# A linear-attention and GLU block: attention pinned in one order, k and v in thirds, single PSUM banks, and a logarithm for the root

## The chip, the cores and the metric

The kernel runs on one core of one Trainium2 chip. The metric is device time in microseconds (us) of one execution.

## The reference

Sequence 2048, model width 576, 32 heads of 18, GLU width 4608, all in fp32:

```python
xn = layernorm(x)                                  # 2048 x 576
q, k, v = split(xn @ wqkv)                         # 32 heads of 18 each
phi = lambda t: jnp.where(t > 0, t + 1, jnp.exp(t)) + 1e-6
pq, pk = phi(q), phi(k)
kv = einsum("bhsd,bhse->bhde", pk, v)              # per head 18 x 18
z = einsum("bhsd->bhd", pk)
o = (pq @ kv) / (pq . z + 1e-6)
s = merge_heads(o) @ wo
glu = (gelu(x1 @ w_gate) * (x1 @ w_up)) @ w_down   # x1 = xn
out = x + s * silu(glu)
```

## The kernel before

**Tiles and words.** The 2048 tokens are 4 blocks of 512 (TBN), each of 4 tiles of 128 (so tiles 0 to 15; `2 * TT` is 8). The width 576 is cut in two halves of 288, a half in two chunks of 128 rows and a rest of 32. Every operand of a big product is held as two words: the high word is a copy rounded to fp32r by ScalarE (Copy), the low word is what is left, subtracted by VectorE or GpSimd. A product of one half then takes the seven matmuls of PASSES (high x high, high x low and low x high of both chunks, and one for the rests).

**Attention, first part.** `moments` (L141) makes mean and 1/sqrt(variance) of one to four tiles: statistics on VectorE, a Sqrt on ScalarE (L153), a reciprocal and one Newton step on VectorE. `center` normalizes a tile in place, `turn` (L169) transposes it on TensorE, six 128x128 pieces into a pair of PSUM banks (xt), `place` (L178) writes the words (xo) and keeps an fp32 copy (xf). k and v of a tile (`k_mm`, `v_mm`, through `mm_x` L315) are 28 matmuls of 288 columns each into a pair of banks (pk, pv). `k_post` forms phi(k): VectorE's minimum, ScalarE's Exp, VectorE's maximum, GpSimd's sum. `v_post` copies v, head group by head group with a column of ones, into va, partly on VectorE and partly on ScalarE, and then runs `kv_mm` (L306) of the tile before, which adds va^T pk of five head groups to the banks kv_a and kv_b. This part, tiles 0 to 7, is written out by hand from L984 on; `fixed[0]` is true, so every engine keeps the order of the program.

**Attention, second part.** From `fixed[0] = False` on, ScalarE, VectorE and TensorE instructions are ordered by the framework's scheduler, not by the program; GpSimd's `pool` and the `dma` calls stay pinned. Here the kernel makes the differences T1 to T4 of the halves of x (for the Winograd products of the GLU), stores their words in DRAM (`keep`), makes q of blocks 0 and 1 (`q_store`, five groups a block, 14 matmuls of 512 columns each at L374, phi, to DRAM), normalizes blocks 2 and 3 (`norm`), makes k and v of tiles 8 to 15, and q of blocks 2 and 3 (`q_hold`, kept on chip). `kv_done` and `kv_wo` fold the output weights wo into kv (kvh, kvl, kv4). `make_sel` writes a selection matrix; `den` (L553) makes the denominators of a block and their reciprocals, `scale` spreads them over the heads with a matmul (b, L565), multiplies q by them (ph, L567) and makes the words pq. `s_mm` (L588) is 28 matmuls of 288 a tile; s goes to DRAM.

**GLU.** `fixed[0]` is true again. 36 matrices (18 gate, 18 up, in turn) each make seven products into eight banks: al, be, ga and de for two blocks at a time (`matrix`, L669 is the matmul of `product`); the words of the next matrix (wa, wb) are cut behind them in the `todo` lists. Then `down_all` makes the down projection in 126 groups of 24 matmuls (bd, L874) from words of h (s, by `prep_s`) and of the down weights (t), with seven Winograd steps into eight banks, and `close` applies silu, multiplies by s, adds x and stores.

**PSUM.** A pool of `n1` single banks and `n2` pairs is opened for each stage: `banks(0, 3)` at first, (2, 2) from the differences on, (4, 2) for the q of block 3 and s, and (8, 0) for the GLU; two more banks hold kv_a and kv_b until (4, 2) is opened.

The helpers `act` (L97), `vec` (L100), `mm` (L103) and `pool` (L106) record most operations, so these four lines stand for many places and the operand names tell them apart.

Of the kernel before, what the change touches and what calls it, by code (L numbers as in the profile page):

```python
# [36 lines left out]
LN_EPS = 1e-5  # L37
EPS = 1e-6
# [12 lines left out]
def block_kernel(ctx, tc, x, xe, wq_d, wkv_d, wo, wgu_d, wd_d, out):  # L51
# [53 lines left out]
    def pool(op, *args):  # L105
        tc.keep_in_program_order(getattr(nc.gpsimd, op)(*args))  # L106
# [4 lines left out]
    def split(hi, lo, src):  # L111
        nc.scalar.activation(hi, src, AF.Copy)
        nc.vector.tensor_sub(lo, src, hi.bitcast(F32))
# [26 lines left out]

    def moments(tb, t0=0, t1=TT):  # L141
        n = t1 - t0
        bn = sb.tile([P, TT, 12], F32, tag="bn", bufs=2, name=f"bn_{tb}_{t0}")
        st = sb.tile([P, 6, TT], F32, tag="st", bufs=4, name=f"st_{tb}_{t0}")
        mv = sb.tile([P, 2 * TT, 2], F32, tag="mv", bufs=4, name=f"mv_{tb}_{t0}")
        for t in range(t0, t1):
            xs = xstat[tb, t // 2 * 2][:, t % 2]
            for j in range(2):
                vec("bn_stats", out=bn[:, t - t0, 6 * j : 6 * j + 6], in_=xs[:, j, 0:HALF])
            vec("bn_aggr", out=mv[:, t - t0, :], in_=bn[:, t - t0, :])  # L150
        sd, v, r, c = (st[:, i, 0:n] for i in range(4))
        var = mv[:, 0:n, 1]
        act(sd, var, AF.Sqrt, bias=eps_t)  # L153
        vec("tensor_scalar", v, var, LN_EPS, None, op0=ALU.add)
        vec("reciprocal", r, sd)
        vec("tensor_mul", c, r, r)
        vec("tensor_mul", c, c, v)
        vec("tensor_scalar", c, c, -0.5, 1.5, op0=ALU.mult, op1=ALU.add)
        vec("tensor_mul", c, c, r)
        for t in range(t0, t1):  # L160
            mom[tb * TT + t] = mv[:, t - t0, 0:1], c[:, t - t0 : t - t0 + 1]

    def center(n):

        xs = xstat[n // TT, n % TT // 2 * 2][:, n % 2]
        m, r = mom.pop(n)
        vec("tensor_scalar", xs, xs, m, r, op0=ALU.subtract, op1=ALU.mult)

    def turn(n):  # L169

        xs = xstat[n // TT, n % TT // 2 * 2][:, n % 2]
        xts[n] = pair(f"xt_{n}")
        for j in range(2):
            for k in range(3):
                c = slice(k * P, (k + 1) * P)
                pin(nc.tensor.transpose(xts[n][:, j, c], xs[:, j, c], ident))  # L176

    def place(n):  # L178

        tb, t = divmod(n, TT)  # L180
        s, b = divmod(tb, 2)
        c = slice(t * P, (t + 1) * P)
        for j, nm in enumerate(BS[b]):
            if t == 0:
                xo[s][nm] = big(2 * b + j, [P, 5, TBN], F32R, f"xo_{s}_{nm}")
            o = xo[s][nm]
            v = xts[n][:, j, 0 : 3 * P].rearrange("p (k t) -> p k t", k=3)
            act(o[:, 0:3, c], v, AF.Copy)
# [20 lines left out]
    def norm(tb):  # L209
        moments(tb)  # L210
        for n in range(tb * TT, tb * TT + TT):
            center(n)
            turn(n)
            place(n)

    def differences(s, eng):
        f = xf[s]
        eng.tensor_sub(f["B11"], f["B12"], f["B11"])
        f["T1"] = f["B11"]
        eng.tensor_sub(f["B12"], f["B22"], f["B12"])  # L220
# [13 lines left out]
    def build(s, nm, i):  # L234
        o = big(i, [P, 5, TBN], F32R, f"xo_{s}_{nm}")
# [5 lines left out]
    wsub = {}  # L241

    NC2 = (Q2, HALF, HALF)

    def w_tiles(mats, first, name):
        n, nc2 = 2 * len(mats), 2 * NC2[mats[0]]
        mains = [big(first + i, [P, 4, nc2], F32R, f"{name}_{i}") for i in range(n)]
        last = big(first + n, [P, n, nc2], F32R, f"{name}_l")
        for i, m in enumerate(mats):
            for j in range(2):  # L250
                wsub[m, j] = (mains[2 * i + j], last[:, 2 * i + j, :])

    def load_w(m, c, j):
        raw = slot([P, 3, HALF], F32, f"rw_{m}_{c}_{j}")
        nc.sync.dma_start(out=raw, in_=wkv_d[2 * m - 2 + c, j])
        return raw

    def load_w2(m, j, i):
        raw = big(i, [P, 2, 3, NC2[m]], F32, f"rw_{m}_{j}")
        src = wq_d[:, j] if m == 0 else wkv_d[2 * m - 2 : 2 * m, j]  # L260
        nc.sync.dma_start(out=raw, in_=src.rearrange("c p k f -> p c k f"))
        return raw[:, 0], raw[:, 1]

    def prep_hi(m, c, j):
        act(wsub[m, j][0][:, 0:3, c * NC2[m] : (c + 1) * NC2[m]], raws[m, c, j], AF.Copy)

    def prep_lo(m, c, j, on_pool):
        main, last = wsub[m, j]
        cs = slice(c * NC2[m], (c + 1) * NC2[m])
        r = slice(2 * KR, 3 * KR)  # L270
        raw = raws[m, c, j]
# [43 lines left out]
    def mm_x(o, m, tb, t, js=(0, 1)):  # L315
        s, b = divmod(tb, 2)
        for j in js:
            for i, (wi, xi, rows) in enumerate(PASSES):
                for c in range(2):
                    mm(  # L320
                        o[:, c, 0:HALF],
                        xo[s][BS[b][j]][0:rows, xi, t * P : (t + 1) * P],
                        w_part(m, j, wi, c * HALF, (c + 1) * HALF, rows),
# [650 lines left out]
    for t in (2, 3):  # L974
        load_stat(0, t)
# [206 lines left out]
```

## Time and profile before

| | |
|---|---|
| runs | 1549.44, 1551.21, 1551.27 us, median 1551.21 |
| the profiled execution | 1550.36 us; span of its instructions 1548.7 us |
| instructions | 22597 |
| mean granted TensorE clock | 0.993 of full speed |
| DMA | 257.36 MB in 112335 packets, mean 166 GB/s |

PE is TensorE's matmul, PEld its weight load, DVE VectorE, ACT ScalarE, POOL GpSimd, SP the engine that issues most DMAs. A row of groups has line, engine, operation, output <- inputs, shapes and count, then busy us and mean ns of one, then the idle time just before these instructions and what ended most of it. A row of waits has engine, what waited, what it waited for, then total us, count and the longest. A row of a timeline has start and length in us and a count. A window's row gives start:end, length, busy time (count) of each engine, the granted clock, the DMA engines' busy share and GB/s. In the order's rows a name ends in the number of its tile.

### The profile page before, as it was taken

To read this page: it belongs to the slowest core of one execution; us is meant where nothing else is said; L and a number is where in the kernel's file an instruction comes from. 1 tells how busy PE (TensorE), PEld (TensorE's weight loads), DVE (VectorE), ACT (ScalarE), POOL (GpSimd) and SP (SyncE) were. 2 spreads that over 40 slices of the span, in tenths; PEclk is the share of its full clock that TensorE was granted. 3 is DMA by queue.
4 is the path that set the end of the run, shared out by engine and by line. 5 is a ranking of instruction groups with operands and counts; after the bars stand their busy time and mean duration, and the time that the engine had idled before them with its cause. 6 is when DMAs were issued, how large, how long until landed. Compare 5 with 4: busy or idle time off the path is not lost.

```text
span 1548.7 us, 22597 instructions
## 1 busy us (share of the span) xinstructions
PE 1507.1 (97%) x8552; PEld 1343.1 (87%) x8552; DVE 1075.0 (69%) x1571; ACT 553.6 (36%) x945; POOL 563.8 (36%) x512
## 2 busy tenths in 40 slices
PE   4989999999999999999999999999999999999998
PEld 4988997888888888888888888888889999999998
DVE  6668336637777887877788787777784666555775
ACT  3435214333222222232232223232335545445443
POOL 4144423023456565444665554456440020000120
PEclk9999999999999999999999999999999999999999
DMA  4327000572344434333444343334569757787872
GB/s 153 135 89 263 4 6 2 184 269 111 133 158 167 167 131 162 120 129 128 165 166 165 133 154 114 133 135 167 197 224 323 248 168 253 246 266 242 285 251 105
DMA packets 112335, 257.36 MB, mean 166 GB/s; under 512 B 10130, under 2 KB 38546, under 8 KB 110178
## 3 DMA queue, kind: packets, MB, share of 16 engines
q1 hardware_dynamic: 110162, 243.07, 44.0%
q0 software_dynamic: 2064, 12.85, 2.3%
q8 instruction: 67, 1.10, 0.3%
q14 instruction: 42, 0.34, 0.1%
HBM read 157.93 MB, written 97.91 MB: 165 GB/s over the span
## 4 chain that ended last, share of the span: by engine, by line
PE 90%; DVE 6%; ACT 2%; DMA 1%; issue 1%; POOL 0%; SPq 0%; ACTq 0%; DVEq 0%; POOLq 0%
PE bd L874 25%; PE al L669 15%; PE de L669 15%; PE ga L669 15%; PE be L669 7%; PE s L588 4%; PE q L374 3%; PE pv L103 2%; PE pk L103 2%; PE kv_a L103 1%; DVE xo_B L100 1%; PE xt L176 1%; PE d L546 1%; DVE x L100 1%; DVE bn L100 1%
## 5 line engine op out<-in xcount | busy, mean ns | idle before, releaser
L874 PE MATMUL bd<-t,s 128*128 128x288 f32 x3024 | 401.4, 295 | 2.2 <-DVE u L100 2.2
L874 PEld LDWEIGHTS bd<-t,s 128*128 128x128 f32 x3024 | 400.9, 188 | 2.8 <-DVE u L100 2.7
L100 DVE TENSOR_TENSOR s<-sr,s 128x512 fp32r<-128x512 f32 x252 | 181.3, 759 | 119.5 <-ACT s L97 115.0
L97 ACT ACTIVATE s<-sr 128x512 fp32r<-128x512 f32 x252 | 149.2, 626 | 192.4 <-PE bd L874 125.4
L106 POOL TENSOR_TENSOR hs<-h,h 128x512 f32<-128x512 f32 x72 | 100.6, 1406 | 232.5 <-DVE h L100 229.6
L97 ACT ACTIVATE h<-h 128x512 f32<-128x512 f32 x108 | 67.0, 633 | 247.9 <-DVE h L100 132.5
L106 POOL TENSOR_TENSOR sx<-sx 128x288 f32<-128x288 f32 x24 | 27.9, 1182 | 318.6 <-DVE sx L100 317.5
L100 DVE TENSOR_TENSOR wa<-raw,wa 128x256 fp32r<-128x256 f32 x72 | 78.2, 1087 | 53.2 <-ACT wa L97 52.0
L106 POOL TENSOR_TENSOR sm<-raw 128x384 f32<-128x384 f32 x72 | 76.1, 1057 | 96.2 <-DMA raw<-in_wgu_dram 73.5
L100 DVE TENSOR_TENSOR h<-h,u 128x512 f32<-128x512 f32 x108 | 97.8, 905 | 3.7
L106 POOL TENSOR_TENSOR td<-td 128x288 f32<-128x288 f32 x72 | 72.4, 1005 | 55.4 <-DMA td<-in_wd_dram 51.1
L97 ACT ACTIVATE wa<-sm 128x1152 fp32r<-128x1152 f32 x36 | 41.8, 1161 | 139.2 <-PE de L669 139.2
L100 DVE TENSOR_TENSOR wa<-sm,wa 128x768 fp32r<-128x768 f32 x72 | 65.3, 907 | 35.7 <-ACT wa L97 34.9
L100 DVE TENSOR_TENSOR wb<-sm,wb 128x256 fp32r<-128x256 f32 x72 | 60.8, 844 | 20.5 <-ACT wb L97 20.0
L97 ACT ACTIVATE u<-al 128x512 f32<-128x512 f32 x72 | 40.9, 593 | 91.1 <-PE al L669 91.1
L100 DVE TENSOR_TENSOR wb<-raw,wb 128x256 fp32r<-128x256 f32 (+1 forms) x108 | 70.0, 648 | 1.7 <-ACT wb L97 0.2
L374 PE MATMUL q<-xo_B,wq 128*128 128x512 f32 x240 | 66.7, 404 | 1.6 <-ACT e_q L97 1.5
L100 DVE TENSOR_TENSOR u<-u,ga 128x512 f32<-128x512 f32 x72 | 49.3, 685 | 21.5 <-PE ga L669 20.4
L669 PE MATMUL al<-xo_B,wa 128*128 128x512 f32 x252 | 63.1, 390 | 0.8 <-ACT s L593 0.8
L669 PE MATMUL al<-xr_B,wa 128*128 128x512 f32 x252 | 63.0, 389 | 0.0
L669 PE MATMUL be<-xo_T,wa 128*128 128x512 f32 x252 | 63.0, 389 | 0.0
L669 PE MATMUL be<-xr_T,wa 128*128 128x512 f32 x252 | 63.0, 389 | 0.0
(176 smaller groups left out, 2973.0 us busy)
## 6 DMA issues: line engine op xcount, KB each, us to landing
sr<-hs SPq DMA_DIRECT2D x252, 256.0 KB
hs<-h SPq DMA_DIRECT2D x68, 512.0 KB
raw<-in_wgu_dram SPq DMA_DIRECT2D x36, 768.0 KB
hs<-hs SPq DMA_DIRECT2D x102, 256.0 KB
td<-in_wd_dram SPq DMA_DIRECT2D x18, 576.0 KB
td<-td SPq DMA_DIRECT2D x18, 576.0 KB
tr<-td SPq DMA_DIRECT2D x16, 576.0 KB
tr<-in_wd_dram SPq DMA_DIRECT2D x12, 576.0 KB
```

Of the source, the lines that this page charges most:

```text
L97: pin(nc.scalar.activation(*args, **kw))
L100: pin(getattr(nc.vector, op)(*args, **kw))
L103: pin(nc.tensor.matmul(*args, **kw))
L106: tc.keep_in_program_order(getattr(nc.gpsimd, op)(*args))
L176: pin(nc.tensor.transpose(xts[n][:, j, c], xs[:, j, c], ident))
L374: nc.tensor.matmul(pq, w_part(0, j, wi, gi * P, (gi + 1) * P, rows), xo[s][nm][0:rows, xi, :], start=(n == 0), stop=(n == 2 * len(PASSES) ...
L546: nc.tensor.matmul(pd[2 * H * i : 2 * H * (i + 1), 0:HB], at["zc"][:, gi, :], ph[tb][:, gi, i * HB : (i + 1) * HB], start=(gi == 0), stop= ...
L588: nc.tensor.matmul(pss[:, c, 0:HALF], pq[:, t * P : (t + 1) * P], kw[:, c * HALF : (c + 1) * HALF], start=(n == 0), stop=(n == len(steps) ...
L669: nc.tensor.matmul(o, w[0:rows, wi, :], xop[0:rows, xi, :], start=(start and n == 0), stop=(n == len(PASSES) - 1), skip_group_check=True,)
L874: nc.tensor.matmul(banks[j][:, 0:HALF], hw[n, s][:, a, t * P : (t + 1) * P], w[:, c, g % 4], start=(new and g == 0 and m == 0), stop=(g == ...
```

## The change

All of attention is written in one pinned order, and `fixed` is gone. In parts:

- **PSUM**: one pool for the whole kernel, six single banks (`bank`) and two more (`own_bank`), which hold the first transposes, then kv_a and kv_b, then al and two of the eight bd.
- **Root**: 1/sqrt(v) is exp(-0.5 ln v), then the same Newton step. `moments` is split in `spread` (statistics, Ln, Exp) and `scales` (the step). The table set that holds both functions is loaded by an instruction at the program's start.
- **Start**: 16 transposes of the identity stand ahead of everything on TensorE. Loads, words and products of tiles 0 and 1 are interleaved anew.
- **k and v** are made together in thirds of 384 columns, each third in one bank: `x_mm(t, c)` is 14 matmuls; the rest rows have a word of their own (KV_PASSES). The copies to va are all on ScalarE. `kv_tile` fixes the order within a tile: the next tile's transposes and words behind the first two thirds, `kv_mm` of the tile before behind the last third, normalizing of the tile after next at the end. `kv_mm(7)` stands behind the first q, `kv_mm(15)` behind the first q of block 2.
- **q of blocks 0 and 1**: behind each of the ten q's a list (`behind`) of what goes on: T4, the words of T1, T3, T2, and x of tiles 8 to 10. For block 3 the minimum in phi is made on ScalarE (Relu(-x), then Exp(-x)).
- **kv_wo** is run group by group between the q's of block 2; the moving of rows between its results has its own step.
- **s**: the words of q of the next block (`den`, `scale`, and now `halve`) are made between the tiles of s of the block before (`aside`); the odd blocks' words have buffers of their own (12 and 14). The words of block 3's and 1's T's and the sums and first words of the first gate matrix are also laid between tiles of s. T3 is read back behind the last s on GpSimd's queue, B21, B22 and T4 on SP's.
- **GLU**: the words wa and wb have exchanged buffers (15 and 14); the call `prep_s(3)`, in the last matrix, is moved from step 5 of the matrix to step 6. At the end `close_last` makes the sum and silu of a tile, and its product, addition and store stand behind the sum of the next; the last tile is done in two parts.
- **Host**: the weights of k and v are cut in three parts of 384 columns.

```diff
-        act(sd, var, AF.Sqrt, bias=eps_t)
...
-        vec("reciprocal", r, sd)
+        act(st[:, 0, 0:n], mv[:, 0:n, 1], AF.Ln, bias=eps_t)
+        act(st[:, 2, 0:n], st[:, 0, 0:n], AF.Exp, scale=-0.5)
...
+    def kv_tile(t, mid_=(), end=()):
+
+        ahead = t % (2 * TT) != 2 * TT - 1
+        x_mm(t, 0)
+        if ahead:
+            turn(t + 1)
+        k_post(t, 0)
+        x_mm(t, 1)
+        if ahead:
+            place(t + 1)
+            save(t + 1)
+        run(list(mid_))
+        k_post(t, 1)
+        v_post(t, 1)
+        x_mm(t, 2)
+        if t - 1 in vas:
+            kv_mm(t - 1)
+        run(list(end))
+        v_post(t, 2)
...
+    behind = {
+        0: [lambda: kv_mm(N0 - 1), lambda: difference(0, 3)],
+        1: [lambda: spread(N0, 2)],
+        2: [lambda: scales(N0), lambda: center(N0)],
+        3: [lambda: form("T1")],
+        4: [lambda: turn(N0), lambda: place(N0)],
+        5: [lambda: form("T3"), lambda: save(N0)],
+        6: [lambda: center(N0 + 1)],
+        7: [lambda: spread(N0 + 2, 2), lambda: scales(N0 + 2)],
+        8: [lambda: form("T2")],
+        9: [],
+    }
+    for i in range(2 * NHG):
+        q_store(*divmod(i, NHG))
+        run(behind[i])
...
+    aside = {
+        (2, 0): [lambda: den(3), lambda: build(1, "T1", X_SLOT["T1"])],
+        (2, 1): [lambda: scale(3, 0, 1), lambda: halve(3, 0, 1)],
+        (2, 2): [lambda: scale(3, 2, 3, 4), lambda: halve(3, 2, 3, 4)],
+        (2, 3): [lambda: build(1, "T3", X_SLOT["T3"]), lambda: load_mat(0), lambda: q_load(1, 8)],
+        (3, 0): [lambda: den(0), lambda: build(1, "T2", X_SLOT["T2"])],
...
+    for tb in (2, 3, 0, 1):
         for t in range(TT):
             s_mm(tb, t)
+            run(aside.get((tb, t), []))
...
-            todo[5] += [lambda: load_t(3), lambda: prep_s(3)]
+            todo[5].append(lambda: load_t(3))
+            todo[6].append(lambda: prep_s(3))
```

What TensorE gets first, before (xt are the transposes of a tile, pk the products of k, wkv the weights' words, xo_B x's words; the number behind tells the tile):

```order
L176 MATMUL xt_135<-ident,x_0_103 128x128 x6
L176 MATMUL xt_176<-ident,x_0_103 128x128 x6
L103 MATMUL pk_191<-wkv_95,xo_B_143 128x288 x10
L103 MATMUL pk_191<-wkv_l,xo_B_143 128x288 x2
L103 MATMUL pk_191<-wkv_95,xo_B_143 128x288 x2
L103 MATMUL pk_206<-wkv_95,xo_B_143 128x288 x10
```

And after (idle are transposes of the identity, kv_0, kv_1 and kv_2 the thirds of k and v):

```order
L1019 MATMUL idle_99<-ident 128x128
L1019 MATMUL idle_100<-ident 128x128
L162 MATMUL xt_0_145<-ident,x_117 128x128 x3
L162 MATMUL xt_1_146<-ident,x_117 128x128 x3
L90 MATMUL kv_0_179<-wkv_71,xo_B_155 128x384 x7
L90 MATMUL kv_0_179<-wkv_72,xo_B_162 128x384 x7
L162 MATMUL xt_0_199<-ident,x_117 128x128 x3
L162 MATMUL xt_1_200<-ident,x_117 128x128 x3
L90 MATMUL kv_0_217<-wkv_71,xo_B_155 128x384 x7
```

Both tiles' transposes stood ahead of the first product; now tile 0's first third stands between them.

The end of tile 7 on TensorE, before (pv_959 is v of tile 7, the four rows of kv_a and kv_b the kv products of tiles 6 and 7, q_0 the first group of q):

```order
L103 MATMUL pv_959<-wkv_98,xo_B_515 128x288 x2
L103 MATMUL kv_a<-pk_873,va_908 127x126 x4
L103 MATMUL kv_b<-pk_873,va_908 73x72
L103 MATMUL kv_a<-pk_953,va_988 127x126 x4
L374 MATMUL q_0_1042<-xo_B_143,wq_100 128x512 x5
```

And after:

```order
L90 MATMUL kv_2_900<-wkv_73,xo_B_532 128x384
L90 MATMUL kv_a<-pk_794,va_825 127x126 x4
L90 MATMUL kv_b<-pk_794,va_825 73x72
L90 MATMUL q_0_930<-xo_B_155,wq_76 128x512 x5
L90 MATMUL q_0_930<-xo_B_155,wq_l 128x512
L90 MATMUL q_0_930<-xo_B_155,wq_76 128x512
L90 MATMUL q_0_930<-xo_B_162,wq_77 128x512 x5
L90 MATMUL q_0_930<-xo_B_162,wq_l 128x512
L90 MATMUL q_0_930<-xo_B_162,wq_77 128x512
L90 MATMUL kv_a<-pk_873,va_896 127x126 x4
```

The kv product of tile 7 stood ahead of the first q and now stands behind it.

VectorE at the end of the last matrix, before (de are the banks of the last product, s the low words of h for the down groups, numbered by the group, t those of down weights):

```order
L100 TENSOR_TENSOR s_2_9150<-sr_0_8993,s_2_9150 128x512 x2
L100 TENSOR_TENSOR u_1_9012<-u_1_9012,de_1_9059 128x512
L100 TENSOR_TENSOR h_1_0_8833<-h_1_0_8833,u_1_9012 128x512
L100 TENSOR_TENSOR u_0_9014<-u_0_9014,de_0_9067 128x512
L100 TENSOR_TENSOR h_0_0_8835<-h_0_0_8835,u_0_9014 128x512
L100 TENSOR_TENSOR t_9219<-tr_9079,t_9219 128x1152
```

And after:

```order
L87 TENSOR_TENSOR u_1_8897<-u_1_8897,de_1_8944 128x512
L87 TENSOR_TENSOR h_1_0_8718<-h_1_0_8718,u_1_8897 128x512
L87 TENSOR_TENSOR u_0_8899<-u_0_8899,de_0_8952 128x512
L87 TENSOR_TENSOR h_0_0_8720<-h_0_0_8720,u_0_8899 128x512
L87 TENSOR_TENSOR s_2_9061<-sr_0_8878,s_2_9061 128x512 x2
L87 TENSOR_TENSOR t_9104<-tr_8964,t_9104 128x1152
```

The words of the third down group stood ahead of the reads of de and now stand behind them.

More of the change, by code (lines that the diff above doesn't have):

```diff
@@ L37 @@
 LN_EPS = 1e-5
+LN_EXP = 6
 EPS = 1e-6
@@ L234, in build @@
     def build(s, nm, i):
-        o = big(i, [P, 5, TBN], F32R, f"xo_{s}_{nm}")
+        xo[s][nm] = o = big(i, [P, 5, TBN], F32R, f"xo_{s}_{nm}")
         to_operand(o, xf[s][nm], full)
         return o
[L241 to L251, printed above, removed]
@@ L267, in prep_lo, with kv_part, load_kv @@
[L267 to L271, printed above, removed]
+    TW = 2 * D // 3
+    KV = [(c, j) for c in range(3) for j in range(2)]
+    wkv = [big(4 + i, [P, 6, TW], F32R, f"wkv_{i}") for i in range(5)]
+    def kv_part(c, j, i):
+        n = KV.index((c, j))
+        return wkv[n][:, i, :] if n < 5 else wkv[i][:, 5, :]
+    raws = {}
+    def load_kv(c, j):
+        n = KV.index((c, j))
+        if n % 2 == 0:
+            raws["kv", n // 2] = big((2, 3, 12)[n // 2], [P, 2, 3, TW], F32, f"rw_{n}")
+        raws[c, j] = raws["kv", n // 2][:, n % 2]
+        dma(out=raws[c, j], in_=wkv_d[c, j])
@@ L313, in kv_mm, with x_mm @@
             )
-    def mm_x(o, m, tb, t, js=(0, 1)):
+    KV_PASSES = [(0, 0), (1, 1), (3, 0), (4, 1), (0, 3), (1, 4), (2, 2)]
+    pkv, pks, vas, es = {}, {}, {}, {}
+    def x_mm(t, c):
+        tb, i = divmod(t, TT)
         s, b = divmod(tb, 2)
[L317 to L323, printed above, removed]
-                        start=(j == 0 and i == 0), stop=(j == 1 and i == len(PASSES) - 1),
-                    )
@@ new lines, in run @@
+    def run(todo, n=None):
+        for _ in range(len(todo) if n is None else min(n, len(todo))):
+            todo.pop(0)()
+    def kv_tile(t, mid_=(), end=()):
[16 more added lines that the diff above has]
+        v_post(t, 2)
@@ new lines, in block_kernel @@
+    first = [own_bank(f"idle_{i}") for i in range(2)]
+    for i in range(16):
+        pin(nc.tensor.transpose(first[i % 2][:, 0:P], ident, ident))
+    load_x(0, 1)
+    load_kv(0, 0)
+    load_kv(0, 1)
+    load_x(1, 1)
+    load_kv(1, 0)
+    load_kv(1, 1)
+    load_x(2, 1)
+    load_kv(2, 0)
+    load_x(3, 1)
+    load_kv(2, 1)
+    spread(0, 1)
+    scales(0)
+    center(0)
+    turn(0, own_bank)
+    kv_hi(0, 0)
+    kv_lo(0, 0, vec, (False,))
+    place(0, (0,))
+    kv_lo(0, 0, vec, (True,))
@@ L1013, in block_kernel, with x_next @@
+    k_post(1, 1)
+    v_post(1, 1)
+    x_mm(1, 2)
+    save(2)
+    v_post(0, 2)
+    center(3)
+    v_post(1, 2)
+    make_masks()
+    def x_next(n):
+        if n % 2 == 0:
+            spread(n, 2)
+            scales(n)
+        center(n)
+    x_mm(2, 0)
+    kv_mm(0)
     turn(3)
-    v_post(0)
-    v_post(1)
+    k_post(2, 0)
+    x_mm(2, 1)
     place(3)
-    load_stat(1)
-    stats(4, 2)
-    center(4)
-    center(5)
-    make_masks()
-    for n in range(2, 2 * TT):
+    save(3)
+    load_x(6, 2)
@@ new lines, in block_kernel @@
+    k_post(2, 1)
+    v_post(2, 1)
+    x_mm(2, 2)
+    kv_mm(1)
+    x_next(4)
+    v_post(2, 2)
+    load_q(0)
+    for n in range(3, 2 * TT):
+        ends = []
+        if n < 2 * TT - 2:
+            ends.append(lambda n=n: x_next(n + 2))
+        if n >= TT:
+            j, c = divmod(n - TT, 2)
+            prep_q(c, j)
+            if n == TT + 1:
+                load_q(1)
+        if n == 2 * TT - 1:
+            ends += [lambda i=i: difference(0, i) for i in range(3)]
+        kv_tile(n, end=ends)
+        if n in (4, 6):
+            load_x(n + 4, 2)
@@ new lines, in block_kernel @@
+    for n in range(N0, 2 * N0):
+        ends = []
+        if n < 2 * N0 - 2:
+            ends.append(lambda n=n: center(n + 2) if n == N0 else x_next(n + 2))
+        if n == N0 + 1:
+            ends.append(lambda: form("T4"))
+        if n == 2 * N0 - 3:
+            ends.append(load_wo)
+        if n == 2 * N0 - 1:
+            ends += [lambda i=i: difference(1, i) for i in range(3)]
+        kv_tile(n, end=ends)
+        if n in (N0, N0 + 2):
+            load_x(n + 4, 2)
+    q_hold(2, 7, [
+        [lambda: kv_mm(2 * N0 - 1), kv_done, lambda: difference(1, 3)],
+        [lambda: kv_wo(4)],
+        [lambda: kv_wo(0), lambda: kv_wo(1), move_rows],
+        [lambda: kv_wo(2), lambda: kv_wo(3)],
+        [make_sel],
+    ])
```

741 lines of the change are left out of this document (351 added, 390 removed).

## The prediction

> **What bounds the kernel now.** First the page's busy row, then the table of busy time by stretches, cut where the stages change.
>
> ```profile
> PE 1507.1 (97%) x8552; PEld 1343.1 (87%) x8552; DVE 1075.0 (69%) x1571; ACT 553.6 (36%) x945; POOL 563.8 (36%) x512
> ```
> ```profile
> core 0: us, PE busy (x) PEld busy (x) DVE busy (x) ACT busy (x) POOL busy (x), PEclk, DMA share, GB/s
> 0.00:8.29 8.29, 0.00 (x0) 0.03 (x1) 2.66 (x10) 2.39 (x3) 1.11 (x8) 1.00 0.72 245
> 8.29:44.03 35.74, 24.38 (x146) 22.95 (x147) 24.40 (x56) 15.75 (x31) 15.29 (x22) 0.95 0.36 136
> 44.03:108.87 64.84, 57.44 (x431) 56.78 (x430) 43.14 (x98) 27.57 (x57) 19.93 (x22) 0.94 0.30 113
> 108.87:165.38 56.51, 54.65 (x280) 46.21 (x279) 43.36 (x84) 28.18 (x51) 19.68 (x18) 0.95 0.51 189
> 165.38:224.99 59.61, 59.61 (x463) 59.61 (x463) 16.44 (x32) 10.42 (x32) 26.23 (x23) 1.00 0.01 4
> 224.99:263.44 38.45, 36.39 (x168) 27.98 (x166) 23.19 (x39) 14.37 (x22) 15.43 (x19) 1.00 0.01 2
> 263.44:338.46 75.02, 73.40 (x525) 66.30 (x523) 45.83 (x66) 31.02 (x49) 12.98 (x15) 1.00 0.53 181
> 338.46:1138.27 799.81, 799.81 (x3529) 662.49 (x3529) 621.46 (x822) 233.82 (x387) 410.60 (x348) 1.00 0.41 150
> 1138.27:1541.95 403.68, 401.45 (x3025) 400.74 (x3023) 251.91 (x361) 189.23 (x314) 42.60 (x41) 1.00 0.72 243
> 1541.95:1548.70 6.75, 0.00 (x0) 0.00 (x0) 2.59 (x7) 0.89 (x2) 0.00 (x0) 0.74 0.18 66
> ```
> TensorE (PE) sets the time. The gate and up products (338.46 to 1138.27) leave no gap, the down products 2.2 us. What can go lies in attention, the first 338.46 us: 8.29 before the first matmul, 11.4 and 7.4 idle in the two stretches after it, and 1.9, 2.1 and 1.6 later; then 6.75 at the very end. PE's waits name the owners.
>
> ```profile
> PE xt L176 <- DVE x L100: 18.4, 3, 8.3
> PE kv_a L103 <- DVE va L100: 5.2, 2, 4.5
> ...
> PE bd L874 <- DVE u L100: 2.2, 2, 1.7
> ```
> The long ones are x not yet normalized when PE reaches the transposes, and va not copied before the kv product that stands ahead of q. Gaps cost more than themselves: matmuls behind one run slowly. In PE's timeline ten of 288 columns take 2.75 us behind the second gap; in a dense stretch 56 go by from 85.43 to 92.96.
>
> ```profile
> 18.55 2.75 PE L103 MATMUL pk<-wkv,xo_B 128*128 128x288 f32 x10
> ...
> 80.08 0.82 PE L176 MATMUL xt<-ident,x 128*128 128x128 f32 x6
> 80.65 1.56 PE L103 MATMUL pv<-wkv,xo_B 128*128 128x288 f32 x10
> ...
> 85.43 1.56 PE L103 MATMUL pk<-wkv,xo_B 128*128 128x288 f32 x10
> ...
> 92.96 1.04 PE L103 MATMUL kv_a<-pk,va 128*127 128x126 f32 x8
> ...
> 93.94 1.57 PE L103 MATMUL pk<-wkv,xo_B 128*128 128x288 f32 x10
> ...
> 119.56 1.52 PE L374 MATMUL q<-xo_B,wq 128*128 128x512 f32 x6
> ...
> 121.15 1.52 PE L374 MATMUL q<-xo_B,wq 128*128 128x512 f32 x6
> ```
> So, start to start and dense: 7.53 us for a tile's k and v (134.5 ns a matmul), 0.98 for its kv product, 0.57 for its transposes, 1.59 for seven of q's matmuls (227 ns).
>
> **Part by part.** *Thirds.* A tile's k and v become 42 matmuls of 384 columns in place of 56 of 288, the same columns. No row shows 384; between 134.5 ns at 288 and 227 at 512 the line gives 174 ns, 7.31 us a tile. By 288's price per column it would be 7.53 (no gain), by 512's 7.15. I take the line, since both ends lie on it.
>
> *Start, to where two tiles are through k and v, four are transposed and tile 0's kv product is run (44.03).*
>
> ```profile
> 3.77 0.82 DVE L100 BATCH_NORM_STATS2 bn<-x 128x6 f32<-128x288 f32 x2 [3.77 <-DMA x<-in_xe_dram]
> ...
> 7.51 0.68 DVE L100 TENSOR_SCALAR x<-x,mv,st 128x768 f32<-128x768 f32 x1
> ```
> ```profile
> 4.92 1.28 ACT L97 ACT_TABLE_LOAD   x1 [4.92 <-DVE mv L100]
> 6.21 0.29 ACT L97 ACTIVATE st<-mv,eps_t 128x1 f32<-128x1 f32 x1
> ```
> ```profile
> L97 ACT ACTIVATE wa<-sm 128x1152 fp32r<-128x1152 f32 x36 | 41.8, 1161 | 139.2 <-PE de L669 139.2
> L100 DVE TENSOR_TENSOR wa<-sm,wa 128x768 fp32r<-128x768 f32 x72 | 65.3, 907 | 35.7 <-ACT wa L97 34.9
> ```
> The table load leaves the path (it now runs while x is on its way) and logarithm and exponential take the place of root and reciprocal: x of tile 0 is centred at about 6.9, not 8.19. [...]
>
> More is won by the order: PE now runs the first third of tile 0 ahead of tile 1's transposes. It needs one 1161 ns word from ACT and x's words, so it starts near 8.4 (bytes are no limit: 245 GB/s over 8.29 us are 2.0 MB, x and both halves of the third 1.6), where pk starts at 18.55. It is then paced by words: by like rows (907 for the low words of a third's half, 0.72 for a placed half tile, 0.82 and 0.68 for statistics and centring), DVE's instructions up to tile 3's centring sum to 19.0, from 6.9 to 25.9 if it never waits. Followed in the order, it waits some 4 us: for the exponential behind ACT's words, and for ACT at each placed half. PE then ends tiles 0 and 1 at about 28, and tile 0's kv product, which waits for ACT's va copies (all of va is ACT's now), at 33.2, plus 0.6 for tile 3's transposes. By then it has also run a third of tile 2 (2.4): 31.4 against 44.03, a gain of **12.6** (17 without DVE's waits, 8 with twice them). The 16 transposes ahead of x (at half the dense pace, 16/6 x 0.57 x 2, about 3 us long) end before x is ready and delay nothing. [...]
>
> *Tiles 2 to 7 (64.84 us).* Dense, before is 6 x 7.53 + 7 x 0.98 + 4 x 0.57 = 54.3; 10.5 are gaps and slow matmuls. Now centring stands two tiles ahead, va is off DVE, and the kv product of tile 7 stands behind the first q, whose 3.2 us cover its copies. A tile's thirds take five banks of six, each read about a tile before its next use. With 7.31 a tile 53.0, and 1 left for new waits: a gain of **10.8** (8.5 to 11.8).
>
> *q of blocks 0 and 1, tiles 8 to 15 (116.1 us).* The trace has 161 of the 280 q matmuls here, the rest later.
>
> ```profile
> 108.87:165.38 56.51, 40.22 (x161) 0.95 0.51 189
> ```
> 161 x 0.227 + 8 x (7.31 + 0.98 + 0.57) = 107.4. DVE is the danger: in the 33 us of ten q's it now gets both their steps (13.7), the forming of T1, T3, T2 (6.7 by two rows of 1359 and 887 ns), statistics, centring, placing and a difference (about 9), and is 90% full.
>
> ```profile
> L100 DVE TENSOR_TENSOR xo_T<-xf_B,xo_T 128x1024 fp32r<-128x1024 f32 x8 | 10.9, 1359 | 6.0 <-ACT xo_T L97 5.9
> L100 DVE TENSOR_TENSOR xo_T<-xf_B,xo_T 32x512 fp32r<-32x512 f32 x8 | 7.1, 887 | 0.1
> ```
> Six banks let it fall some 6 us behind before PE waits; followed in the order it ends 7 late, for about 1 of wait. Gain **7.7** (4 to 9).
>
> *q of blocks 2 and 3, and s (113.5 us).* The same work in another order. Of the 3.7 idle some goes, and new waits come: in the order ACT's copies of the selection wait for POOL's masks, and what is queued behind them (q's relu) runs about 4 us late, covered by the banks; the last words of block 2 come about 1 late; the first sums by the selection wait for the reciprocal.
>
> ```profile
> L554 DVE RECIPROCAL r<-r 128x256 f32<-128x256 f32 x4 | 7.0, 1753 | 0.1
> ...
> L559 DVE TENSOR_TENSOR aux<-r,aux 32x256 fp32r<-32x256 f32 x8 | 4.8, 599 | 1.9 <-ACT aux L558 1.7
> ...
> L558 ACT ACTIVATE aux<-r 64x256 fp32r<-64x256 f32 x8 | 3.3, 414 | 3.4 <-DVE r L554 3.2
> ```
> From den's end an addition (put at 0.4), 1.75 + 0.41 + 2 x 0.6 and hand-overs are about 4.2, beside a tile of s (28 matmuls of 288 at 134.5 ns, 3.77): 0.5, three times. I set this stage to **0** (-4 to +3). On the queues, T3 comes back only when the last s ends, since it gets the slot of the high words; it is needed 22 us later, and at 181 GB/s, s's own rate, 1.3 MB take 7. The weights of the second matrix come about 8 us into the first, needed at 44. Neither is on the path.
>
> *Down's first banks and the end.*
>
> ```profile
> 1137.18 3.48 DVE L100 TENSOR_TENSOR s<-sr,s 128x512 fp32r<-128x512 f32 x2
> ```
> ```profile
> 1543.72 0.45 DVE L100 TENSOR_TENSOR u_d<-u_d,bd 128x288 f32<-128x288 f32 x1
> ```
> The words of 3.48 us now stand behind the reads of de, so the 2.2 us wait goes, but the words of the third group then have less cover: **1.2** (0 to 2.2). At the end DVE ran 1.8 behind PE (1543.72 against 1541.95); with each tile's product put behind the next tile's sum it keeps up, but the last tile's steps are split in two: **0.9** (0.5 to 1.2).
>
> **Sum**: 12.6 + 10.8 + 7.7 + 0 + 1.2 + 0.9 = 33.2. The profiled execution took 1550.36 (1548.7 of span), so 1517.2; the median before, 1551.21, is 0.85 higher. I say 1517.
>
> **Rivals.** (a) DVE or ACT, now in one written order, fall behind in the q's and at the start: the low ends of these terms, 8 + 8.5 + 4 + 1 = 21.5, so 1529. For it: 90% of DVE; against it: six banks.
> (b) The middle doesn't gain: thirds in single banks bring waits as long as those removed. Only start and end remain, 1550.36 - 14.7 = 1536. Against it: five banks a tile, and the dense 59.61 stretch, where three pairs were enough.
> (c) Slower: the words of a block, made during s of the one before, come only when that s is over. A block's chain is 3.8 from den to the reciprocal's words and five times 2.0 for product, copy and subtraction (0.68, 0.63, 0.69), about 14; three blocks 41, fully exposed 1517 + 41 = 1558. It decides against the change from 34 exposed. Against it: s of a block is 15 long and DVE is busy 45.8 of 75.
>
> ```profile
> L567 DVE TENSOR_TENSOR ph<-ph,b 128x512 f32<-128x512 f32 x20 | 12.7, 680 | 13.8 <-PE b L565 13.7
> L112 ACT ACTIVATE pq<-ph 128x512 fp32r<-128x512 f32 x16 | 9.8, 629 | 6.8 <-DVE ph L567 6.8
> L113 DVE TENSOR_TENSOR pq<-ph,pq 128x512 fp32r<-128x512 f32 x16 | 10.4, 685 | 1.2 <-ACT pq L112 1.2
> ```
> (d) The change doesn't do what it says: table loads remain between logarithm and exponential. The order shows one load ahead of attention and none in it, so this gets no more than 0.01.
>
> **Chances.** Forecast 0.70, (a) 0.20, (b) 0.05, (c) 0.04, (d) or no change 0.01. The range takes the forecast's ends, from 1508 (start 17, middle 9, no new waits) to 1530, which holds (a). Over 0.2% (3 us, about what a measurement of this kernel can tell from no change) faster: all but (c) and (d).
>
> **What would show it.** First matmul of k before 10 us; tile 2 begun by 31; no wait for x over 1 us behind that; kv_a without its 4.5 us; gate at about 307, not 338.46; no bd wait over 1. A gate start past 325, or PE waits for words in s of several us a block, would make the prediction wrong.

## The result and the profile after

The changed kernel took 1512.33 us (median of 1512.12 to 1513.18), against 1550.99 (1549.44 to 1551.27) before: a ratio of 0.9754, 95% interval 0.9737 to 0.9771. The forecast was 1517 with a range of 1508 to 1530. The profiled execution took 1512.12. The first lines of its page:

```profile
span 1510.4 us, 22223 instructions
...
PE 1497.7 (99%) x8344; PEld 1337.9 (89%) x8344; DVE 1068.7 (71%) x1568; ACT 555.5 (37%) x1008; POOL 543.9 (36%) x499
```

Busy time by stretches, cut at tile 0's kv product, the first q, the first q of block 2, the first matrix, the first down group and the last matmul:

```profile
0.00:33.33 33.33, 26.59 (x133) 24.73 (x134) 24.37 (x55) 15.90 (x33) 13.30 (x23) 0.90 0.47 177
33.33:85.88 52.55, 52.46 (x339) 52.14 (x339) 26.98 (x70) 24.60 (x71) 20.47 (x25) 1.00 0.44 159
85.88:190.13 104.25, 104.25 (x607) 98.41 (x606) 68.40 (x145) 40.57 (x102) 30.30 (x33) 1.00 0.27 104
190.13:303.50 113.37, 113.30 (x722) 99.69 (x720) 69.94 (x106) 48.51 (x95) 24.59 (x31) 1.00 0.29 105
303.50:1103.20 799.70, 799.70 (x3531) 662.16 (x3529) 623.90 (x827) 235.79 (x391) 412.65 (x351) 1.00 0.41 152
1103.20:1505.25 402.05, 401.37 (x3025) 400.77 (x3023) 252.74 (x360) 189.59 (x315) 42.60 (x41) 1.00 0.71 244
1505.25:1510.40 5.15, 0.00 (x1) 0.00 (x0) 2.40 (x8) 0.54 (x2) 0.00 (x0) 1.00 0.26 86
```

From 33.33 to the down products TensorE's list has no wait left. What it still waits for is in the first 16 us and once in the down stage:

```profile
PE xt L162 <- DVE x L87: 2.8, 1, 2.8
...
PE bd L908 <- DVE s L87: 0.7, 1, 0.7
PE kv L90 <- POOL wkv L93: 0.3, 1, 0.3
PE kv L90 <- ACT xo_B L84: 0.3, 1, 0.3
```

TensorE's timeline gives the marks of the start and the price of a third:

```profile
8.05 2.77 PE L90 MATMUL kv<-wkv,xo_B 128*128 128x384 f32 x9 [0.25 <-ACT xo_B L84]
...
28.36 5.13 PE L90 MATMUL kv<-wkv,xo_B 128*128 128x384 f32 x28
33.33 1.45 PE L90 MATMUL kv_a<-pk,va 128*127 128x126 f32 x8
...
35.32 5.13 PE L90 MATMUL kv<-wkv,xo_B 128*128 128x384 f32 x28
40.29 1.05 PE L90 MATMUL kv_a<-pk,va 128*127 128x126 f32 x8
...
41.27 2.70 PE L90 MATMUL kv<-wkv,xo_B 128*128 128x384 f32 x14
43.81 0.82 PE L162 MATMUL xt<-ident,x 128*128 128x128 f32 x6
44.38 5.13 PE L90 MATMUL kv<-wkv,xo_B 128*128 128x384 f32 x28
```

Start to start, 28 matmuls of 384 take 4.97 and 14 take 2.54: 7.51 for a tile, where 56 of 288 took 7.53. To compare stages, both kernels are cut at equal work (a third of tile 2, 2.5, is behind the mark of the start now; the kv products of tiles 7 and 15, 0.98 each, stand behind the q that follows; 161 q matmuls stood in the third stage of the table before, 140 now, and 21 x 0.228 is 4.8):

| stage | before | after, equal work | gain | forecast |
|---|---|---|---|---|
| start | 44.03 | 35.32 - 2.5 = 32.8 | 11.2 | 12.6 |
| tiles 2 to 7 | 64.84 | 50.56 + 2.5 + 0.98 = 54.0 | 10.8 | 10.8 |
| q of blocks 0 and 1, tiles 8 to 15 | 116.12 | 104.25 + 4.8 = 109.0 | 7.1 | 7.7 |
| q of blocks 2 and 3, s | 113.47 | 113.37 - 4.8 - 0.98 = 107.6 | 5.9 | 0 |
| gate and up | 799.81 | 799.70 | 0.1 | 0 |
| down | 403.68 | 402.05 | 1.6 | 1.2 |
| behind the last matmul | 6.75 | 5.15 | 1.6 | 0.9 |
| sum | | | 38.3 | 33.2 |

### The profile page after: what moved, and what is told of

Same layout as the page of the kernel before. It is cut to its first block, busy times and chain, and to the rows that moved or that the text cites. A ratio compares the mean times of both kernels' runs of the same rounds, so it can differ in the third digit from the quotient of the medians.

```text
span 1510.4 us, 22223 instructions
## 1 busy us (share of the span) xinstructions
PE 1497.7 (99%) x8344; PEld 1337.9 (89%) x8344; DVE 1068.7 (71%) x1568; ACT 555.5 (37%) x1008; POOL 543.9 (36%) x499
## 4 chain that ended last, share of the span: by engine, by line
PE 96%; DVE 2%; DMA 1%; ACT 0%; issue 0%; SPq 0%; DVEq 0%; ACTq 0%
PE bd L908 26%; PE al L703 15%; PE de L703 15%; PE ga L703 15%; PE be L703 8%; PE kv L90 7%; PE q L90 4%; PE s L90 4%; PE kv_a L90 1%; PE xt L162 1%; PE d L90 1%; DMA rw<-in_wkv_dram 1%; DVE s L87 0%; PE kw L90 0%; PE b L90 0%
## 5 line engine op out<-in xcount | busy, mean ns | idle before, releaser
L90 PE MATMUL kv<-wkv,xo_B 128*128 128x384 f32 x672 | 126.4, 343 | 0.6 <-POOL wkv L93 0.3
L90 PEld LDWEIGHTS kv<-wkv,xo_B 128*128 128x128 f32 x672 | 118.0, 191 | 1.9 <-POOL wkv L93 0.9
```

What stands on the lines that cost most here:

```text
L90: pin(nc.tensor.matmul(*args, **kw))
```

## The experiments

Twelve kernels ran. The kernel before, run beside them, had medians of 1550.85 to 1551.22, so times of different groups compare within some 0.4 us. Where stages are given they are read from each kernel's timeline.

**The logarithm alone, and the root back.** In before:

```diff
-        act(sd, var, AF.Sqrt, bias=eps_t)
+        act(sd, var, AF.Ln, bias=eps_t)
+        act(r, sd, AF.Exp, scale=-0.5)
...
-        vec("reciprocal", r, sd)
...
+    pin(nc.scalar.add_instruction(mybir.InstLoadActFuncSet(
...
```

> The kernel before with one part alone: exp(-0.5 ln v) for root and reciprocal, and the table set loaded at the start. My theory (what was won in attention comes from what stands ahead of what in each engine's order; the table loads paid little) says 3 to 4.5 us faster than before, so 1546.5 to 1548: 1.3 at the first tile, 1.1 to 1.3 of the 4.53 that the kv product of tile 7 waited, 0.7 at tile 8. The rival (the table loads were what held ScalarE, and VectorE behind it) says 8 us or more, about 1541, with the kv wait of 4.53 nearly gone.

Measured: 1549.75 (1546.12 to 1550.22), ratio 0.9989 (0.998 to 0.9998): 1.1 faster, less than either theory said. The first q starts 3.06 earlier (105.81 for 108.87), but the GLU only 0.66 (337.80 for 338.46). Two rows of its timeline show why:

```profile
104.95 1.18 PE L104 MATMUL kv_a<-pk,va 128*127 128x126 f32 x4 [4.30 <-DVE va L101]
154.38 0.46 PE L104 MATMUL kv_a<-pk,va 128*127 128x126 f32 x2 [2.27 <-DVE va L101]
```

The wait of tile 7 keeps 4.30 of 4.53, though no table is loaded there any more, and at tile 8 one of 0.71 becomes 2.27. In before's VectorE timeline the copies of va stand behind the whole normalizing of block 2, which the scheduler had put ahead of them:

```profile
103.29 3.41 DVE L100 TENSOR_SCALAR x<-x,mv,st 128x768 f32<-128x768 f32 x4
106.62 0.41 DVE L100 COPY va<-pv 128x252 f32<-128x252 f32 x1
```

And the other way round, in the changed kernel, without the load at the start:

```diff
-        act(st[:, 0, 0:n], mv[:, 0:n, 1], AF.Ln, bias=eps_t)
-        act(st[:, 2, 0:n], st[:, 0, 0:n], AF.Exp, scale=-0.5)
+        act(st[:, 0, 0:n], mv[:, 0:n, 1], AF.Sqrt, bias=eps_t)
...
+        vec("reciprocal", st[:, 2, 0:n], st[:, 0, 0:n])
...
-    pin(nc.scalar.add_instruction(mybir.InstLoadActFuncSet(
...
```

> The changed kernel with root and reciprocal back and no load at the start. My theory: 1.3 at the first tile and a little more where VectorE is 90% full behind the first q's, 2 to 5 us slower, 1514 to 1517. Rival (the table loads held the middle): 8 us or more slower, above 1520, with waits of TensorE for x or va in every pair of tiles.

Measured: 1514.09 (1513.92 to 1514.5), 1.8 slower, just under what I expected and far from the rival. The first q starts 1.7 later (87.56 for 85.88), the GLU 2.0 (305.46 for 303.50). So 1.7 of the 2.0 is lost ahead of the first q and 0.3 behind it.

**The transposes of the identity** taken out:

```diff
-    for i in range(16):
-        pin(nc.tensor.transpose(first[i % 2][:, 0:P], ident, ident))
```

> The changed kernel without the 16 transposes of the identity at the start. My theory: the first products are paced by their words, so no more than 0.6 us either way, 1511.7 to 1513. Rival (the transposes lift the granted clock for the first third): 1.5 to 2.5 us slower.

Measured: 1512.08 (1511.96 to 1512.24): nothing. Thirteen of the first products take 4.68 without them, nine 2.77 with them; tile 0's kv product starts at 33.63 and 33.33. The pace of the first third doesn't count: TensorE waits for x of tile 1 behind it either way, 1.53 without the transposes and 2.78 with them, until 15.73 and 15.50.

**GpSimd beside VectorE at the start.** In the changed kernel, VectorE and GpSimd ahead of the wait of 2.8:

```profile
11.99 1.67 DVE L87 SCALAR_TENSOR_TENSOR st<-st 128x1 f32<-128x1 f32 x1
13.70 0.16 DVE L87 TENSOR_TENSOR st<-st 128x1 f32<-128x1 f32 x1
13.89 0.84 DVE L87 SCALAR_TENSOR_TENSOR st<-st 128x1 f32<-128x1 f32 x1
14.77 0.68 DVE L87 TENSOR_SCALAR x<-x,mv,st 128x768 f32<-128x768 f32 x1
```
```profile
11.62 3.10 POOL L93 TENSOR_TENSOR wkv<-rw,wkv 128x768 fp32r<-128x768 f32 x2 [0.51 <-ACT wkv L84]
```

The row of the second fence ends its two subtractions at 14.72, and the last short step of VectorE ends at 14.73.

```diff
-    kv_lo(1, 0, pool)
...
     center(1)
+    kv_lo(1, 0, vec)
     kv_hi(1, 1)
```

> The changed kernel with the low words of the second third's first half (of k and v's weights) made on VectorE behind the normalizing of tile 1, not on GpSimd ahead of it. In the changed kernel two of VectorE's instructions of 128x1 (scalar_tensor_tensor) take 1.67 and 0.84 us there, 0.16 elsewhere, and end when GpSimd's subtraction ends. My theory (they wait for GpSimd's instruction to end): both fall to 0.16, TensorE's wait of 2.78 for x of tile 1 falls to about 0.4, and the kernel gets 1.5 to 2.4 us faster, 1510 to 1511. Rival (VectorE is simply full, and more work on it costs time): 0 to 1.5 us slower.

Measured: 1510.38 (1510.17 to 1510.56), ratio 0.974 (0.9727 to 0.9753) to before: 1.95 faster than the changed kernel, and the fastest of all that ran. Its VectorE and TensorE:

```profile
12.39 0.16 DVE L87 SCALAR_TENSOR_TENSOR st<-st 128x1 f32<-128x1 f32 x1
...
12.78 0.16 DVE L87 SCALAR_TENSOR_TENSOR st<-st 128x1 f32<-128x1 f32 x1
```
```profile
13.71 0.88 PE L162 MATMUL xt<-ident,x 128*128 128x128 f32 x6 [0.85 <-DVE x L87]
...
23.89 2.70 PE L90 MATMUL kv<-wkv,xo_B 128*128 128x384 f32 x14 [1.41 <-DVE pk L87]
```

x of tile 1 comes 1.8 earlier, with more work on VectorE, not less. TensorE's waits alone don't give the gain. From the end of the first third to the products behind tile 2's transposes it takes 15.63 in the changed kernel and 14.13 here, for the same matmuls; of these 2.78 and 2.51 (0.85, 0.25, 1.41) are waits. So 1.2 of the 1.5 is the pace of the matmuls:

```profile
15.50:18.92 3.42, 3.42 (x12) 0.50 0.21 53
```
```profile
15.50:18.92 3.42, 3.42 (x21) 1.00 0.65 224
```

(The first row is the changed kernel's, the second this one's; the columns here and in the like rows below are length, TensorE busy and count, granted clock, DMA share and GB/s.) Behind the wait of 2.78 the clock was halved for 3.4 us; behind the 0.85 it was not. 1.41 is still lost to a bank not yet read. Two attempts at that followed. First the steps that free the bank, and the last third's low words, ahead of the statistics of tiles 2 and 3:

```diff
-    spread(2, 2)
     kv_lo(2, 0, vec)
+    k_post(0, 0)
+    spread(2, 2)
...
-    k_post(0, 0)
```

> The kernel of after_lo_dve (low words of the second third's first half on VectorE behind the normalizing of tile 1), with phi's two steps on tile 0's first third and the low words of the last third put ahead of the statistics of tiles 2 and 3 on VectorE. In after_lo_dve TensorE waited 1.41 for the bank that these two steps free. Theory: that wait goes and nothing takes its place, 1.0 to 1.4 us faster than after_lo_dve's 1510.4, so 1509.0 to 1509.4. Rival (x of tiles 2 and 3 then comes late): the same 1510.4, with a wait for x at the transposes of tile 2.

Measured: 1512.51 (1511.49 to 1513.45). The wait for pk went, and others came: the last third's low words, on GpSimd behind a ScalarE copy that the logarithm of tiles 2 and 3 now held up. Behind them the clock was 0.50 from 25.93 to 29.34, so waits no longer in sum than after_lo_dve's came out 2.1 slower.

```profile
PE kv L90 <- POOL wkv L93: 1.4, 3, 0.8
```

Then with that copy ahead of the logarithm and those low words on VectorE:

```diff
     kv_lo(2, 0, vec)
+    kv_hi(2, 1)
     k_post(0, 0)
+    kv_lo(2, 1, vec)
     spread(2, 2)
     x_mm(0, 1)
-    kv_hi(2, 1)
-    kv_lo(2, 1, pool)
```

> The kernel of after_start, in which TensorE waited for GpSimd's low words of the last third, because ScalarE made their high words only behind the logarithm of tiles 2 and 3. Now the high words of the last third stand ahead of that logarithm on ScalarE, and all low words of that third are VectorE's (1.6 us more there, ahead of the statistics of tiles 2 and 3). Theory: the waits for the last third go, x of tile 2 is ready at about 25.6, where TensorE would want it at 25.0 (26.4 in after_lo_dve): 0.5 to 0.9 faster than after_lo_dve's 1510.4, so 1509.5 to 1509.9. Rival (the start is bound by VectorE's whole work, which this raises): 1510.4 to 1511.5, with a wait for x of tile 2 of over 1.5.

Measured: 1511.38 (1510.98 to 1511.51), 1.0 slower than after_lo_dve. The last third's low words on VectorE put off the statistics, and x of tile 2 is ready at 26.56, not at 25.6. The transposes of tile 2, which could start at 25.13, start at 26.81, the last to come being banks that ScalarE reads behind the same logarithm:

```profile
PE xt L162 <- ACT xf_B L84: 1.7, 1, 1.7
```

The time is the rival's, and so, nearly, is the wait. ScalarE's copies only add the last 0.25 of 1.7: without them the transposes would still wait 1.4 for x, and VectorE works from 16.90 until that x is done with one gap of 0.4. So at this point VectorE's work, which the edit raised, holds TensorE.

**The order within attention.** The kv products of tiles 7 and 15 ahead of the q that follows:

```diff
+    kv_mm(N0 - 1)
...
-        0: [lambda: kv_mm(N0 - 1), lambda: difference(0, 3)],
+        0: [lambda: difference(0, 3)],
...
+    kv_mm(2 * N0 - 1)
     q_hold(2, 7, [
-        [lambda: kv_mm(2 * N0 - 1), kv_done, lambda: difference(1, 3)],
+        [kv_done, lambda: difference(1, 3)],
```

> The changed kernel with the kv products of tiles 7 and 15 ahead of the first q that follows each, as before the change for tile 7. In the changed kernel's trace va of tile 7 is there at 85.72 and phi of k at 86.35, and the product would stand at 85.88. Theory (the 4.53 of before came from what VectorE and ScalarE did ahead of va, not from this place): a wait of 0.5 at each place and a slow restart at most, 0.5 to 2 us slower, 1512.8 to 1514.3. Rival (the place is what removed the wait): 4 us or more slower at tile 7 alone.

Measured: 1513.34 (1513.27 to 1514.28), 1.0 slower, with

```profile
PE kv_a L90 <- POOL va L93: 0.7, 2, 0.4
```

so the place is worth 0.4 to 0.5 each. What removed the 4.53 is what stands ahead of va: its copies are all ScalarE's now, and the normalizing of block 2 stands behind the first q's. Which of these two did it was not run apart. The words of q not made during s of another block, shown for block 3 (blocks 0 and 1 likewise):

```diff
-        (2, 0): [lambda: den(3), lambda: build(1, "T1", X_SLOT["T1"])],
-        (2, 1): [lambda: scale(3, 0, 1), lambda: halve(3, 0, 1)],
-        (2, 2): [lambda: scale(3, 2, 3, 4), lambda: halve(3, 2, 3, 4)],
-        (2, 3): [lambda: build(1, "T3", X_SLOT["T3"]), lambda: load_mat(0), lambda: q_load(1, 8)],
+        (2, 0): [lambda: build(1, "T1", X_SLOT["T1"])],
+        (2, 3): [lambda: den(3), lambda: scale(3, 0, 1), lambda: halve(3, 0, 1),
+                 lambda: scale(3, 2, 3, 4), lambda: halve(3, 2, 3, 4),
+                 lambda: build(1, "T3", X_SLOT["T3"]), lambda: load_mat(0), lambda: q_load(1, 8)],
```

> The changed kernel with the denominators and words of a block's q (blocks 3, 0 and 1) made behind the last tile of s of the block before, not between its tiles. The prediction's rival (c) priced this at 14 us a block, 41 in all, 1553. Worked out anew from the changed kernel's rows: about 3.8 to the reciprocal's words and 1.37 of VectorE for each of five groups, of which the first tile of s hides some 3, so 9 to 11 a block: 27 to 33 us slower, 1539 to 1545. A rival to both (VectorE is ahead anyway and little is exposed): under 10 us.

Measured: 1531.79 (1531.49 to 1531.86), 19.5 slower, between both ranges: 6.5 a block. TensorE's waits, and the stretches around the first such place:

```profile
PE b L90 <- DVE aux L87: 11.1, 3, 3.7
```
```profile
250.07:253.73 3.66, 0.00 (x1) 0.90 0.61 210
253.73:258.00 4.27, 4.27 (x13) 0.50 0.00 0
258.00:262.00 4.00, 4.00 (x25) 0.77 0.00 0
262.00:275.39 13.39, 13.38 (x104) 1.00 0.79 286
```

The wait to the reciprocal's words is 3.7, as priced (3.8). The five groups' products and words are hidden by b and the first tile of s, but the granted clock is 0.50 and 0.77 in the 8.3 us behind the wait, which costs another 0.50 x 4.27 + 0.23 x 4.00 = 3.1 at the first place. At the other two it was 0.50 for 3.4 us (280.33 to 283.74 and 304.22 to 307.64), which costs 1.7 each. The same written code, handed to the scheduler from the first q to the end of s (`pool` and `dma` stay pinned):

```diff
-    pin = tc.keep_in_program_order
+    fixed = [True]
+    hold = tc.keep_in_program_order
...
+    def pin(ins):
+        if fixed[0]:
+            hold(ins)
...
     N0 = 2 * TT
+    fixed[0] = False
...
+    fixed[0] = True
     for q in range(NQ):
```

> The changed kernel, its code and buffers as they are, but from the first q to the end of s the instructions of TensorE, VectorE and ScalarE are ordered by the framework's scheduler, as before, and no longer pinned. My theory (the written order is what removed the waits between q and the GLU, where I had forecast no gain and 5.9 came): waits of TensorE come back, 3 to 12 us slower, 1515 to 1524. Rival (single banks, buffers and the split into small steps removed them, and any order does): within 1.5 us of 1512.3.

Measured: 1513.7 (1513.46 to 1514.59), 1.4 slower: the rival's bound, so pinning itself is worth little. That any order would do isn't shown, since TensorE's came out the same but for four matmuls; on VectorE the scheduler pulled statistics and normalizing forward again. Two waits came back, both in s:

```profile
239.06 0.79 PE L95 MATMUL s<-kv,pq 128*128 128x288 f32 x4 [1.15 <-DVE pq L92]
243.94 0.73 PE L95 MATMUL b<-aux 128*128 128x512 f32 x2 [0.83 <-DVE aux L92]
```

**The end.** The close as before, sum, silu, product, addition and store of a tile in one go:

```diff
-    def close_last(sx, t, y, p, parts):
+    def close_last(sx, t, y, parts=1):
...
-            vec("tensor_add", y[:, c], y[:, c], p[:, c])
...
-            late += close_last(sx[6][j // TT], j % TT, u[:, j], accs[j], 2 if j == 2 * TT - 1 else 1)
-            run(late, len(late) - 1)
-        run(late)
+            vec("tensor_add", u[:, j], u[:, j], accs[j][:, 0:HALF])
+            run(close_last(sx[6][j // TT], j % TT, u[:, j]))
```

> The changed kernel with the last eight tiles closed as before: sum, silu, product, addition and store of a tile in one go, the last tile not in two parts. Theory: VectorE falls behind TensorE again, the tail behind the last matmul goes from 5.2 back to 6.7, so 1.3 to 1.7 us slower. Rival (the tail is the last store's way to DRAM, and the order of the steps ahead of it is worth little): under 0.6.

Measured: 1513.99 (1513.29 to 1514.41), 1.7 slower; the tail is 6.50 for 5.15. The words of the third group back at their old place:

```diff
-            todo[5].append(lambda: load_t(3))
-            todo[6].append(lambda: prep_s(3))
+            todo[5] += [lambda: load_t(3), lambda: prep_s(3)]
```

> The changed kernel with the words of the third down group again ahead of the reads of the last product's banks. Theory: the wait of 2.2 for those banks comes back and the 0.7 for the words goes, 1.2 to 1.7 us slower. Rival (one wait takes the other's place): within 0.4.

Measured: 1515.28 (1515.19 to 1516.31), 3.0 slower, more than expected. The down stage takes 405.21, the waits being the old ones:

```profile
1107.24 0.67 PE L908 MATMUL bd<-t,s 128*128 128x288 f32 x3 [0.52 <-DVE u L87]
1109.62 20.61 PE L908 MATMUL bd<-t,s 128*128 128x288 f32 x142 [1.71 <-DVE u L87]
```
```profile
1109.00:1114.00 5.00, 4.38 (x21) 0.66 0.43 147
```

Before, the same two waits (0.52 and 1.71) were followed by 32 matmuls in such 5 us at a clock of 1.00, here by 21 at 0.66: the rest of the cost is the clock (0.34 x 4.4 = 1.5). The last section shows how these waits fall differently in the two kernels. Both end edits of the change, and no other, in before:

```diff
+    def close_last(sx, t, y, p, parts):
...
+            late += close_last(sx[6][j // TT], j % TT, u[:, j], accs[j], 2 if j == 2 * TT - 1 else 1)
+            run(late, len(late) - 1)
+        run(late)
...
-            todo[5] += [lambda: load_t(3), lambda: prep_s(3)]
+            todo[5].append(lambda: load_t(3))
+            todo[6].append(lambda: prep_s(3))
```

> The kernel before with the two edits at its end alone: the words of the third down group behind the reads of the last product's banks, and the last tiles' product, addition and store behind the next tile's sum. Theory: both are worth there what the traces give, 403.7 to 402.1 for the down stage and 6.7 to 5.2 for the tail, so 3.0 to 3.3 us faster than before, 1547.6 to 1547.9. Rival (undone alone in the changed kernel they cost 3.0 and 1.7, the first with a lower granted clock behind the wait, so that they are worth 4.7 anywhere): 1546.2.

Measured: 1547.44 (1546.12 to 1548.36), ratio 0.9978 (0.9969 to 0.9987), 3.5 faster; down 402.05 for 403.68, tail 5.31 for 6.75. Its stages give 1.63 + 1.44 = 3.1, close to the 3.2 of the two traces and not the 4.7 of the undoings; the interval alone, 2.0 to 4.8, would not tell these apart.

## Why the prediction was right, and where its terms were not

The gain exceeds the forecast by 5.1. The stage that was put at 0 gave 5.9; all the others together came out 0.8 short.

**Start (12.6, measured 11.2).** x centred at 6.85 (forecast 6.9), first third at 8.05 (8.4). That the kv product stands at 33.33 (33.2) is luck. I had tiles 0 and 1 done at about 28 and the product waiting for va; they were done at 30.9, a third of tile 2 ran up to 33.33, and the product had no wait in the list. What came late was x of tile 1: I counted VectorE's steps at their rows' price, while its short steps ended only with GpSimd's subtractions, 2.2 us on the path (1.67 and 0.84 for 0.16), and the clock fell to 0.50 behind the wait of 2.78; after_lo_dve showed both. Tile 3 was centred at 32.9, not at 25.9 plus 4 of waits. The 1.4 that the stage lacks is a slip in the sum: 33.2 + 0.6 - 2.4 = 31.4 has tile 3's transposes but not the kv product that begins at 33.2, and it took 1.42 (0.98 in a dense stretch). The table load's share stood: 1.3 forecast (x centred at 6.9 for 8.19), 1.2 in before_log's first transposes (7.05 for 8.29), 1.8 in all in after_root.

**Tiles 2 to 7 (10.8, measured 10.8)**, by two errors that cancel. The thirds cost 7.51 a tile, not 7.31: by the column, as at 288, the end of my bounds that gave no gain. The 1 us left for new waits was not needed.

**q and tiles 8 to 15 (7.7, measured 7.1).** No wait came (1 forecast), and the thirds cost 8 x 0.2 = 1.6 more. VectorE, busy for 27.55 of the 33.64 us of ten q's (82%, where I had 90), did not make TensorE wait once: rival (a) fell there, and (b) with it.

**q of blocks 2 and 3, s (0, measured 5.9)** is the term that was mis-sized, beyond its bound of 3. I set the 3.7 us of idle off against new waits (words about 1 late, the reciprocal 0.5 three times); none came, since `den` and the words stand a tile or more ahead of their use. The remaining 2.2 is TensorE's pace between small gaps, which I had not counted: start to start, with the listed idle taken out, q took 242 ns before and 236 after, b 296 and 245, den 124 and 115. after_free gives back 1.4 of it, so most is due to what the code puts between what, and not to the pinning; which of its edits it is was not taken apart.

**Rival (c).** Its mechanism is real, its price was more than twice too high: 6.5 a block, not 14.

**Down and end (1.2 and 0.9, measured 1.6 and 1.6).** The mechanisms were right; the third group's words cost 0.68 of wait in their new place. What the split of the last tile in two does by itself was not run.

**The idle transposes** were priced at nothing ahead of x, and cost and bring nothing.

## What to carry to other kernels

Where one engine is the bound and waits in short gaps, look at what stands ahead of the missing operand on the engine that makes it, before the operation itself: here the cheaper function was worth 1 to 2 us of attention's 35. The rest is the order, the single banks and the steps moved between engines together; they were not run apart. Count a gap's price as the gap and the slow matmuls behind it (3.7 cost 6.5). A step taken off VectorE and given to GpSimd can delay VectorE by more than it frees: here by 2.2 us, where the same two subtractions take 1.51 on VectorE in after_lo_dve.

## What the hardware showed beyond that

**VectorE's short steps beside GpSimd's subtractions.** Two SCALAR_TENSOR_TENSOR steps of 128x1 took 1.67 and 0.84 us while GpSimd subtracted, and GpSimd's subtractions of 128x768 and 32x384 took 3.10 there together. The slow steps ended at 13.67 and 14.73, GpSimd's two instructions at 13.65 and 14.72. The changed kernel has 18 such steps on st, of 128x1 and 128x2: five started while a two-input instruction ran on GpSimd, took 0.81 to 1.67 and ended 0.01 to 0.02 behind it; the other thirteen took 0.15 to 0.16. after_lo_dve, which takes GpSimd's work away from the first two, gives 0.16 for both.

**The clock behind a gap.** In after_words_late the granted clock was 0.50 for 3.41 us behind a gap of 3.72 without a matmul; in the changed kernel it was 0.50 behind the wait of 2.78 too. In the traces of the two kernels the clock changes only at steps of 3.41 us, in the changed kernel at 8.68, 12.09, 15.50 and 18.92. Counted in such steps, the waits of 0.52 and 1.71 fall into one step in after_preps3, which holds 1.55 us of matmuls and is followed by 0.50:

```profile
1107.09:1110.50 3.41, 1.55 (x9) 1.00 0.84 305
1110.50:1113.91 3.41, 3.41 (x17) 0.50 0.28 112
```

In before the same two waits fall into two steps, with 2.44 and 2.17 us of matmuls, and the clock stays:

```profile
1139.03:1142.45 3.42, 2.44 (x17) 1.00 0.34 138
1142.45:1145.87 3.42, 2.17 (x16) 1.00 0.51 174
1145.87:1149.28 3.41, 3.41 (x28) 1.00 0.61 234
```

Of the other steps of the two kernels at a clock of 1.00 in which under 2 us of matmuls ran, those with 1.71 and 0.63 in the changed kernel (from 5.26 and 12.09) and with 0.85, 1.22, 1.26, 1.70 and 0.14 in before (from 29.70, 46.77, 101.38, 152.58 and 1541.81) were followed by 0.50. Those with 1.53 in the changed kernel (from 1503.72, the last matmuls) and 1.94 in before (from 241.33) were not, nor were the two of before's start (0.93 from 5.81, 0.59 from 9.22). So in these runs what a short gap costs hung also on how it fell into the steps.
